# Issuing the last batch's output rows inside the branch's other arm

## The chip, the cores and the metric

The kernel runs on one core of a Trainium2 chip. The metric is the time of one execution on the device, in microseconds, as the median of several runs. A core has five engines with an instruction queue each: PE (matmul), DVE (vector), ACT (scalar), POOL (GpSimd) and SP, which here only issues transfers. The engines wait for each other through semaphores, counters that an instruction or a transfer raises when it is done.

## What is computed

Attention in which a query sees only the keys of its own cluster, followed by an MLP mixer over tokens and channels, all in float32; 4 batches, 8 heads, 768 tokens, 64 values for a head, 16 clusters, 256 hidden values over tokens, 1536 over channels:

```python
q_assign = np.argmax(np.einsum('bhsd,hcd->bhsc', q_n, c_n), axis=-1)
k_assign = np.argmax(np.einsum('bhsd,hcd->bhsc', k_n, c_n), axis=-1)
mask = q_assign[:, :, :, None] == k_assign[:, :, None, :]
scores = np.where(mask, scale * np.matmul(q, k.transpose(0, 1, 3, 2)), -1000000000.0)
...
x = attn_out.transpose(0, 2, 1, 3).reshape(B, S, H * D)
h = np.maximum(x.transpose(0, 2, 1) @ w_tok1, 0.0) @ w_tok2
u = x + h.transpose(0, 2, 1)
return u + np.maximum(u @ w_ch1, 0.0) @ w_ch2
```

## The kernel before

The kernel has a fast path and a general one. The fast path takes shortcuts that hold only for inputs like those given (each query and key with one clear nearest cluster, sums of exponentials within bounds); it checks this while it runs. `fits` and `fits_count` leave three counts in a small tile, `fits_load` (L1000) loads them into registers of every engine, and their sum is `both`. When the fast path's program has ended, each engine compares `both` with 3 * 128 at L1382. If it is smaller, the engine falls through into the code of `general()`, which computes the whole output again in a plain way: some thousands of instructions, 383 of them on SP. Otherwise it jumps over them into the other arm. In the kernel before that arm is empty in the source. The framework still puts instructions there: each engine waits until its own counters have the value of the fast path's end and raises them to the value that the general path would have left, so that what follows can wait for the same numbers. For SP these are eight waits, one for each of the eight counters of its transfers. Then all engines come to the program's end (shown under L1407), where SP waits for all transfers and all engines, and the engines exchange two rounds of semaphores.

The fast path works through the attention for pairs of heads, then through the token part of the mixer for pairs of batches, then through the channel part for one batch after the other, in the order 0, 2, 3, 1. The channel part of a batch has three parts; each has a product up (`ch1_pair`, L799, L812) and a product back down (`ch2_chunks`, L952), both in Winograd's form with seven products of blocks. `by_turns` goes through the products of a part in an order written out by hand: a product on PE into a PSUM bank, then an add on DVE (L565) of that bank onto the batch's tile `xs[b]`. That tile holds 128 partitions with six rows (`j` of 0 to 5) of 512 values each, so that one row is 256 KB over all partitions. The output goes out by rows: `out_row(j)` at L962 issues one transfer from SP.

For the first three batches the six rows are issued together after the third part. For the last batch, which is batch 1, `by_turns` calls `done` after each add; where the product was `c12` or `c21`, the add was the last one to that row, and `done` issues the row. The order of the products at the end is c12 0, c12 1, c11 2, c12 2, c22 0, c22 1, c21 0, c22 2, c21 1, c21 2, so the rows are done as 0 to 5 and the sixth with the last add of the program. SP, whose queue runs in order, thus has at the end: the loads of the counts, six issues that each wait for an add, the comparison and the branch.

The registers are loaded for the last part only, ahead of its `ch2_chunks`; on SP that is right after the third batch's rows.

The tile of the last batch lies in the pool `xpool`. It is opened on the stack `fast`, which is closed ahead of the branch so that the general path can use the space.

Of the kernel before, what the change touches and what calls it, by code (L numbers as in the profile page):

```python
# [19 lines left out]
P = 128  # L20
NJ = S // P
DM = H * D
# [5 lines left out]
HJ = NJ // 2  # L28
# [22 lines left out]
def kernel(  # L51
# [29 lines left out]
    nc = tc.nc  # L81
# [5 lines left out]
    def pool(name, bufs, stack=None, **kw):  # L87
        return (stack or fast).enter_context(
            tc.tile_pool(name=name, bufs=bufs, reuse_waits="tile", **kw)
        )  # L90
# [2 lines left out]
    ps_sc_stack = fast.enter_context(ExitStack())  # L93
    ps_sc = pool("ps_sc", 3, ps_sc_stack, space=PSUM)

    xpool = pool("xpool", 1)
    wc1pool = pool("wc1pool", 1)
    tokens = fast.enter_context(ExitStack())
    x1pool = pool("x1pool", 1, tokens)
# [34 lines left out]
    xs = [(x1pool if b == 1 else xpool).tile([P, NJ, DM], F32, name=f"x{b}") for b in range(B)]  # L134
# [386 lines left out]
    def ptile(tag, n):  # L521

        if tag == "Y":
            return ps_av.tile([P, n], F32, tag="av", name="pY")
        return pools["ps_m"].tile([P, n], F32, tag=tag, name="p" + tag)
# [38 lines left out]
    def add(dst, a, b):  # L564
        nc.vector.tensor_tensor(out=dst, in0=a, in1=b, op=ALU.add)  # L565
# [171 lines left out]
    def between(n=1):  # L737
        if late:
            late.pop(0)()
        for _ in range(min(n, len(others))):  # L740
            others.pop(0)()

    def by_turns(n, product, of, done=None, last=False, after=()):


        if last:
            order = "p1 0 p1 1 p1 2 p5 0 p5 1 p5 2 c11 0 c11 1 u2 0 u2 1 u2 2 c12 0 c12 1 c11 2 c12 2 "
            order += "c22 0 c22 1 c21 0 c22 2 c21 1 c21 2"
        else:
            order = "p1 0 p1 1 p1 2 p5 0 p5 1 p5 2 c11 0 c11 1 u2 0 u2 1 u2 2 c12 0 c12 1 "  # L750
            order += "c22 0 c22 1 c22 2 c12 2 c11 2 c21 0 c21 1 c21 2"
        order = order.split()
        banks, after = {}, dict(after)
        for m in range(len(order) // 2):
            name, i = order[2 * m], int(order[2 * m + 1])
            tag, a, r, to = SEVEN[name]
            if name in FIRST:
                banks[tag, i] = ptile(tag, n)
            product(banks[tag, i], a, r, i, name in FIRST)
            x = of(to, i)  # L760
            add(x, banks[tag, i], x)
            if done:
                done(name, i)
            if m in after:
                after[m]()
            between()

    def tok2_chunks(b, after=()):

        A, R = pools["AT"], pools["RT"]  # L770

        def product(psum, a, r, i, start):
            nc.tensor.matmul(  # L773
                psum, lhsT=A[a][:, i], rhs=R[r], start=start, stop=True,
                skip_group_check=not start,
            )

        def of(to, i):
            return xs[b + int(to[2]) - 1][:, HJ * (int(to[1]) - 1) + i]

        by_turns(DM, product, of, after=after)

    def ch1_pair(part, sets, beside):
# [147 lines left out]
        else:  # L931
            sum_1()

            def late_(i):
                product(X[i], "A22", "T4", i, False)
                nc.scalar.activation(out=a12[:, i], in_=X[i], func=ACT.Relu)
                if i == 0:
                    sub(h2["S2"], h2["S1"], a11)
                else:
                    sum_3()  # L940
                    sum_4()

            late_(0)
            late.append(lambda: late_(1))

    def ch2_chunks(b, part, last, after=()):

        h2, Bw = pools["h2"], pools["B"]

        def product(psum, a, w, i, start):  # L950
            for k in range(2):
                nc.tensor.matmul(  # L952
                    psum, lhsT=h2[a][:, k, i * P : (i + 1) * P], rhs=Bw[w][:, part + 3 * k],
                    start=start and k == 0, stop=k == 1, skip_group_check=not start,
                )

        def of(to, i):
            r, c = int(to[1]) - 1, int(to[2]) - 1
            return xs[b][:, HJ * r + i, 256 * c : 256 * c + 256]

        def out_row(j):
            nc.sync.dma_start(out[b].rearrange("(p j) m -> p j m", p=P)[:, j], xs[b][:, j])  # L962

        def done(name, i):
            if name in ("c12", "c21"):
                out_row(i + HJ * (name == "c21"))

        by_turns(DM // 2, product, of, done if last else None, last, after)
        if part == 2 and not last:
            for j in range(NJ):  # L970
                out_row(j)

    good = const.tile([P, 3], F32, name="good")
    count = const.tile([1, 3], I32, name="count")
# [22 lines left out]
    def fits_load():  # L997

        loaded = [
            nc.values_load(count[0:1, i : i + 1], min_val=0, max_val=P) for i in range(3)  # L1000
        ]
        return loaded[0] + loaded[1] + loaded[2]
# [155 lines left out]
    batches = (0, 2, 3, 1)  # L1158
    for n, b in enumerate(batches):
        turning = []  # L1160
        for part in range(3):
            first, last = n == 0 and part == 0, n == B - 1 and part == 2
# [15 lines left out]
            if last:  # L1178
                both = fits_load()
            after = {}  # L1180
            if part == 2 and not last:
                after[3] = lambda: take(turning, len(turning))
                after[15] = lambda: next(usums)
                usums = u_sums()
            ch2_chunks(b, part, last, after)
            between(len(others))
            if n == 0 and part < 2:
# [191 lines left out]
        gctx.close()  # L1379

    fast.close()
    with tc.If(both < 3 * P):  # L1382
        general()
# [1 line left out]
_INS = ['q', 'k', 'v', 'centroids', 'moe_w_tok1', 'moe_w_tok2', 'moe_w_ch1', 'moe_w_ch2']  # L1385
_OUTS = [((B, S, DM), 'float32')]
# [25 lines left out]
```

## Time and profile before

| what | value |
|---|---|
| median of 4 runs | 829.24 us (828.43 to 829.69) |
| device time of the profiled execution | 829.55 us |
| its span, from the first to the last instruction | 827.7 us |
| mean granted TensorE clock | 0.999 |
| output transfers from L962 | 24 of 256 KB each, median 2.5 us to landing |
| last six issues on SP, start of the first and the last | 813.94, 821.71 us |
| issue time of these six: shortest, median, longest | 332, 333, 1010 ns |
| their landing times: shortest, median, longest | 2.0, 2.0, 3.0 us |

The profiled execution is one run; its device time holds the span and 1.85 us around it. In lines of the profile a small q behind an engine's name (SPq, DVEq) means its sequencer: register, branch, semaphore and transfer-issuing instructions, which don't count as busy time. A group "x8: 17/17/17, 825.8 to 826.3" has eight instructions, shortest, median and longest duration in ns, and the starts of the first and the last in us from the span's start. "DMA to landing" is the time from the start of a transfer's issue to the last increment of its counter. A line of waits reads: who waited, for whom, us in total, times, longest.

### The profile page before, as it was taken

Reading aid. Unit: us, or ns where it says so; the run is one execution under the profiler, and the core shown is the slowest. Engines: PE = TensorE matmul, PEld = TensorE weight load, DVE = VectorE, ACT = ScalarE, POOL = GpSimd, SP = SyncE. Lnnn points to the kernel's source line nnn. Section 1 sums busy time; section 2 is a strip of 40 time slices with the busy share of each in tenths; the row PEclk is TensorE's granted clock in tenths of the full one; section 3 lists DMA queues with packets and bytes.
Section 4 is the critical chain, followed back from the end, with each engine's and each line's share of the span. In section 5 each row is a group of like instructions: output and inputs, shape, how many; then the busy total and the mean of one; then the engine's idle time right before and its main releaser. Section 6 shows DMA issues by size and latency. Waiting matters only on the chain.

```text
span 827.7 us, 11453 instructions
## 1 busy us (share of the span) xinstructions
PE 818.3 (99%) x4282; PEld 526.4 (64%) x4282; DVE 605.2 (73%) x1124; ACT 381.4 (46%) x562; POOL 30.7 (4%) x28
## 2 busy tenths in 40 slices
PE   8999999999999999999999999999999999999996
PEld 4444444444444444444688787878878788787875
DVE  6879898989898968859777687654677456674654
ACT  5588777787878775136202253121541214512020
POOL 1001010111101000000000000000000000000000
PEclk9999999999999999999999999999999999999999
DMA  9797665767676434143000114000130001400002
GB/s 154 140 164 143 128 141 121 157 141 155 139 155 142 84 96 121 51 156 48 0 1 1 29 34 168 1 0 15 35 105 1 1 1 31 122 1 0 1 2 80
DMA packets 184256, 63.39 MB, mean 77 GB/s; under 512 B 172800, under 2 KB 176896, under 8 KB 183936
## 3 DMA queue, kind: packets, MB, share of 16 engines
q1 hardware_dynamic: 182592, 62.18, 34.7%
q8 instruction: 35, 0.57, 0.3%
q10 hardware_dynamic: 1600, 0.39, 0.2%
q14 instruction: 29, 0.24, 0.1%
HBM read 36.21 MB, written 7.86 MB: 53 GB/s over the span
## 4 chain that ended last, share of the span: by engine, by line
PE 95%; DVE 4%; ACT 0%; issue 0%; ACTq 0%; DVEq 0%
PE sc L413 19%; PE av L455 15%; PE pX L952 14%; PE pX L799 11%; PE pZ L952 7%; PE ph L534 5%; PE pY L812 4%; PE pY L952 4%; PE pZ L799 3%; PE pZ L812 3%; PE pX L773 2%; PE pX L812 2%; PE small L491 2%; PE pZ L773 1%; PE small L304 1%; DVE hA L565 1%
## 5 line engine op out<-in xcount | busy, mean ns | idle before, releaser
L437 ACT ACTIVATE ex<-sc 128x768 f32<-128x768 f32 x192 | 151.0, 812 | 27.2 <-PE sc L413 15.5
L413 PE MATMUL sc<-qkT 64*128 64x384 f32 x768 | 155.3, 483 | 0.0
L445 DVE TENSOR_TENSOR sum<-sum,ex 128x768 f32<-128x768 f32 x128 | 127.8, 998 | 27.5 <-ACT ex L437 15.4
L455 PE MATMUL av<-ex,va 128*64 128x384 f32 x768 | 127.4, 488 | 0.0
L565 DVE TENSOR_TENSOR x<-pX,x 128x256 f32<-128x256 f32 (+1 forms) x168 | 76.0, 459 | 40.9 <-PE pX L952 40.4
L455 PEld LDWEIGHTS av<-ex,va 128*64 128x64 f32 x768 | 53.7, 137 | 71.7 <-issue 67.2
L413 PEld LDWEIGHTS sc<-qkT 64*128 64x128 f32 x768 | 67.8, 187 | 38.3 <-issue 38.0
L839 ACT COPY hA<-pX 128x384 f32<-128x384 f32 x24 | 11.5, 479 | 146.0 <-PE pX L799 146.0
L565 DVE TENSOR_TENSOR hA<-pY,hA 128x192 f32<-128x192 f32 (+1 forms) x90 | 36.7, 408 | 50.0 <-PE pY L812 36.0
L821 ACT ACTIVATE hA<-hA 128x768 f32<-128x768 f32 x35 | 29.5, 843 | 87.1 <-DVE hA L565 87.1
L799 PE MATMUL pX<-uT,wc 128*128 128x384 f32 x192 | 67.9, 487 | 0.0
L413 PE MATMUL sc<-ohT 64*128 64x384 bf16 x384 | 62.4, 323 | 0.0
L799 PEld LDWEIGHTS pX<-uT,wc 128*128 128x128 f32 x192 | 35.8, 190 | 17.5 <-issue 0.4
L462 ACT COPY avrows<-av 128x768 uint16<-128x768 uint16 x32 | 25.6, 799 | 44.0 <-PE av L455 44.0
L565 DVE TENSOR_TENSOR x<-pZ,x 128x256 f32<-128x256 f32 (+1 forms) x84 | 36.4, 455 | 11.9 <-PE pZ L952 11.9
L534 PE MATMUL ph<-x,wt 128*128 128x512 f32 x96 | 41.6, 593 | 0.0
L413 PEld LDWEIGHTS <-ohT 64*128 64x128 bf16 x384 | 18.7, 94 | 33.8 <-issue 9.6
L952 PE MATMUL pX<-wc,hA 128*128 128x256 f32 x144 | 36.9, 380 | 0.4 <-ACT hA L897 0.4
L708 ACT COPY uT<-ucols 128x768 uint16<-128x768 uint16 x32 | 33.2, 1050 | 4.5 <-DMA ucols<-urows 4.5
L952 PE MATMUL pY<-wc,hA 128*128 128x256 f32 x144 | 35.1, 379 | 0.0
L952 PE MATMUL pZ<-wc,hS 128*128 128x256 f32 x144 | 35.0, 379 | 0.0
L799 PE MATMUL pX<-uTs,w1s 128*128 128x384 f32 x96 | 34.9, 486 | 0.0
(178 smaller groups left out, 1266.2 us busy)
## 6 DMA issues: line engine op xcount, KB each, us to landing
raw<-in_moe_w_ch_dram SPq DMA_DIRECT2D x24, 512.0 KB, 4.4
va<-in_v_dram SPq DMA_DIRECT2D x16, 384.0 KB, 3.5
out_dram<-x SPq DMA_DIRECT2D x24, 256.0 KB, 2.5
qk<-in_k_dram SPq DMA_DIRECT2D x60, 96.0 KB, 3.9
qk<-in_q_dram SPq DMA_DIRECT2D x60, 96.0 KB, 3.5
raw<-in_moe_w_tok_dram SPq DMA_DIRECT2D x3, 512.0 KB, 4.3
raw<-in_moe_w_tok_dram SPq DMA_DIRECT2D x4, 384.0 KB, 4.1
spill<-x SPq DMA_DIRECT2D x1, 1536.0 KB, 5.1
```

The costliest lines, as they stand in the source:

```text
L413: nc.tensor.matmul(sc[:, h, 0:HS], lhsT=src[rows, 1, j], rhs=src[rows, 0, HJ * qh : HJ * qh + HJ], start=start, stop=not start,)
L437: nc.scalar.activation(out=ex, in_=sc[:, :, 0:HS], func=ACT.Exp, scale=SM_SCALE)
L445: nc.vector.tensor_tensor(out=acc, in0=acc if j > 1 else st["ex", qh, 0], in1=st["ex", qh, j], op=ALU.add)
L455: nc.tensor.matmul(av[h * D : (h + 1) * D], lhsT=st["va"][:, h, j], rhs=ex[:, h], start=(j == 0), stop=(j == NJ - 1),)
L462: nc.scalar.copy(out=st["rows"][:, qh], in_=av.bitcast(U16).rearrange("p (t w) -> p w t", w=2))
L534: nc.tensor.matmul(pf, lhsT=W["tok1"][:, j, t * P : (t + 1) * P], rhs=xs[b][:, j], start=(j == 0), stop=(j == NJ - 1),)
L565: nc.vector.tensor_tensor(out=dst, in0=a, in1=b, op=ALU.add)
L708: nc.scalar.copy(out=out, in_=pools.pop(("ucols", i)).rearrange("p w j t -> p w (j t)"))
L799: nc.tensor.matmul(psum, lhsT=A[a][:, k, c], rhs=R[r][:, k], start=start and k == 0, stop=k == 1, skip_group_check=not start,)
L812: nc.tensor.matmul(psum, lhsT=left[which][a][:, part * P : part * P + P], rhs=right[which][r], start=start, stop=True, skip_group_check=no ...
L821: nc.scalar.activation(out=x, in_=x, func=ACT.Relu)
L952: nc.tensor.matmul(psum, lhsT=h2[a][:, k, i * P : (i + 1) * P], rhs=Bw[w][:, part + 3 * k], start=start and k == 0, stop=k == 1, skip_grou ...
```

## The change

The six row transfers of the last batch no longer stand in the fast path's program between the adds. They stand in the arm of the branch that is taken when the fast path's checks held. `done` and the test of the product's name go away, `out_row` becomes a function of batch and row, and the pool of the last tile is kept open until the end of the kernel, so that the tile may still be read in the arm. The general path, when it runs, writes all four batches itself, as before.

In the built program, SP's part before the branch is shorter by twelve instructions (six transfers, six waits), and its arm grows from 9 instructions to 21. For each row the arm has a wait that raises the row's counter to the other arm's value, less what the row itself will add, then the wait on the same counter, then the transfer, which waits for the same count of DVE's adds as before. Two waits for the two counters that no row uses follow. At the program's end SP's first of eight waits is for the counter of the sixth row and, as before, its sixth asks for DVE's counter too, which DVE raises in its own arm.

```diff
-    xpool = pool("xpool", 1)
+    xpool = pool("xpool", 1, ctx)
...
-    def by_turns(n, product, of, done=None, last=False, after=()):
+    def by_turns(n, product, of, last=False, after=()):
...
-            if done:
-                done(name, i)
...
+    def out_row(b, j):
+        nc.sync.dma_start(out[b].rearrange("(p j) m -> p j m", p=P)[:, j], xs[b][:, j])
+
...
-        def out_row(j):
-            nc.sync.dma_start(out[b].rearrange("(p j) m -> p j m", p=P)[:, j], xs[b][:, j])
-
-        def done(name, i):
-            if name in ("c12", "c21"):
-                out_row(i + HJ * (name == "c21"))
-
-        by_turns(DM // 2, product, of, done if last else None, last, after)
+        by_turns(DM // 2, product, of, last, after)
         if part == 2 and not last:
             for j in range(NJ):
-                out_row(j)
+                out_row(b, j)
...
-    with tc.If(both < 3 * P):
+    with tc.If(both < 3 * P) as fit:
         general()
+    with fit.Else():
+
+        for j in range(NJ):
+            out_row(batches[-1], j)
```

## The prediction

> **What bounds the kernel now.** I read the page's first two parts, to see which engine fills the span and at which clock.
>
> ```profile
> span 827.7 us, 11453 instructions
> PE 818.3 (99%) x4282; PEld 526.4 (64%) x4282; DVE 605.2 (73%) x1124; ACT 381.4 (46%) x562; POOL 30.7 (4%) x28
> PEclk9999999999999999999999999999999999999999
> ```
>
> TensorE is busy for 99% of the span, at a granted clock that stays in the top tenth in every slice. The change touches no matmul and no vector instruction; in the built changed program the four compute engines have, ahead of the branch, the same instructions in the same order with the same waits and the same addresses. So nothing before the last stage can move. What can move is the end: TensorE is done near 821.2, the span ends at 827.7, and the 6.5 us between them belong to something else. So next I read the chain of waits of the last stretch and its timeline.
>
> ```profile
> 816.04 5.20 PE pX L952 x24
> 821.23 0.02 issue
> 821.26 0.42 DVE x L565
> ...
> 813.94 8.78 SPq L962 DMA_DIRECT2D out_dram<-x  x6
> ...
> 821.71 1.01 SPq L962 DMA_DIRECT2D out_dram<-x  x1
> ```
>
> The chain ends with the last add on DVE (821.26 to 821.68). Its row, the sixth, is issued by SP at 821.71. That issue holds SP for 1.01 us; the page's view of this line gives 332 to 333 ns as minimum and median of the six. Then the line of the branch itself, and what SP waited for.
>
> ```profile
> L1382 SPq EVENT_SEMAPHORE  x8: 17/17/17, 825.8 to 826.3; - x8
> L1382 PEldq COMPARE_BRANCH  x1: 3779/3779/3779, 820.1 to 820.1; - x1
> L1382 DVEq COMPARE_BRANCH  x1: 72/72/72, 821.4 to 821.4; - x1
> L1382 SPq COMPARE_BRANCH  x1: 58/58/58, 822.9 to 822.9; - x1
> L1382 PEldq EVENT_SEMAPHORE  x1: 51/51/51, 823.9 to 823.9; - x1
> L1382 DVEq EVENT_SEMAPHORE  x1: 21/21/21, 824.3 to 824.3; - x1
> ...
> SPq L1382 <- SPq L1382: 2.9, 1, 2.9
> ...
> L1407 SPq EVENT_SEMAPHORE  x8: 27/28/28, 826.4 to 826.8; - x8
> ...
> DMA to landing us min/median/max: 2.8/2.8/2.8
> ```
>
> This is the bound of the tail. SP compares and jumps at 822.9, and its first instruction in the arm that is taken comes at 825.8: for 2.9 us it waits for nothing but itself. The same gap stands behind the branches of DVE (821.4 to 824.3, 2.9), PE (820.1 to 823.9, 3.8, booked as the branch's own time) and ACT (806.4 to 808.8, 2.4); on POOL, with the shortest program, it is 0.5 (467.7 to 468.2). I read it as the time to load the code of a far target. Meanwhile the sixth row, issued at 821.71 and landing 2.8 us later (last line), has been in memory since 824.5. SP then does eight waits in the arm (825.8 to 826.3), eight at the program's end (826.4 to 826.8) and the closing exchange between the engines, which ends at 827.7. So SP, not the row, sets the end: the jump starts only when the last row has been issued.
>
> **The change, part by part.**
>
> *The six issues move behind SP's branch.* They are the same six transfers of 256 KB in the same order, each waiting for the same count of DVE's adds. What they are moved past is SP's two branch instructions; no other queue is passed, and behind SP's last load of the counts (716.7, all done by about 717.2 on SP) nothing else stands on SP in this program. So SP can jump at about 717.3. The first row is wanted at 813.94. A code load of 2.9 us, or PE's 3.8, would be over by 721.1, which leaves 92 us of cover. That cover is the work of the last batch on PE; without it the first row would be late by the 2.9 us.
>
> *What the arm adds.* Ahead of each row stand a wait that also raises the row's transfer counter to what the other arm would have left, and the wait that was there before. A wait with such a raise takes about 0.07 us from start to start in the trace (eight in 825.8 to 826.3). The fifth issue ends at 821.2 (820.84 and 0.33), the sixth starts at 821.7: two waits, 0.15 us, fit into that half microsecond while DVE does the last add. So they cost nothing; with no gap they would cost 0.15.
>
> *What is taken off the path.* After the sixth issue (end 822.7) SP has two more catch-up waits (0.15) and reaches the program's end at about 822.9. There the first of the eight waits is the one on the sixth row's counter. SP stands there until that row has landed, and the rest of the tail follows as now: from the first of these waits to the end of the span it took 827.7 - 826.4 = 1.3 us. The landing thus takes the place of the code load as what SP waits for last.
>
> *The price of the landing.* It is in the trace: 821.71 + 2.8 = 824.5. From below: the shortest of the last six took 2.0, which would be 823.7. From above: the longest, the fifth row, took 3.0, which would be 824.7. The fast ones had issues of 0.33 us and no other load around; the fifth and the sixth lie inside PE's and DVE's code loads, which stay where they are. So I take the 2.8 of the very same transfer and keep both ends.
>
> *The next engine in line.* Of the eight last waits, the sixth also asks for DVE's mark, and DVE makes it in its own arm at 824.3, after its own jump. That jump cannot go earlier, since it stands behind the last add. In the present run SP's sixth wait is at about 826.7 (826.4 and five steps of 0.06). So even a row that lands at once cannot bring more than 826.7 - 824.35, about 2.35 us. PE's mark, at 823.9, is behind that.
>
> *The pool in another stack.* `xpool` now lives until the kernel's end, so the six rows may still be read in the arm. In the built program the addresses of the main part are unchanged; the general path reuses less memory, and that path doesn't run. Cost nothing.
>
> **The sum**, on the profiled execution: first end wait from 826.4 to 824.5, that is 1.9 us; 0.1 off for the step from the counter's last increment to the wait and for rounding, so 1.8. Span 827.7 to 825.9; device time 829.55 to 827.75. That execution lies 0.31 above the median of the runs (829.24), so the median goes to 827.4, 0.22% less.
>
> The row says that a jump costs 2.9 us on SP, 58 ns for the instruction and the rest for what follows. [...]
>
> [...]
>
> **Rivals.**
>
> *DVE becomes the last one.* The sixth issue took 1.01 us instead of 0.33. If that came from SP's own state before the jump, the row lands by 823.7 to 824.0, and DVE's mark at 824.3 decides. For it: five of six issues took 0.33. Against it: the issue falls into PE's code load (820.1 to 823.9), as does the fifth row with its 3.0 us. Gain 2.35: 826.9.
>
> *A second code load at the end.* If the code behind the arm isn't there yet, SP pays the load again after the sixth issue: 822.7 + 0.15 + 2.9 = 825.8 instead of 826.4, a gain of 0.6, time 828.6. Against it: in this trace SP goes from its arm (last wait 826.3) to the end (826.4) without a gap, and it has 92 us to load ahead. That the change doesn't do what it says (SP not jumping early) would leave 829.2; the order of the built program speaks against it, so I put it in with this case.
>
> *The slower side.* The arm's code is loaded in pieces, a piece ends just before the sixth row, and the next is fetched only when SP gets there. Then the issue starts at 821.2 + 2.9 = 824.1 and the row lands 2.0 to 3.0 later, at 826.1 to 827.1, against the present first end wait at 826.4: with 2.8, 826.9, which is 0.5 slower, 829.7; with PE's load of 3.8 another 0.9, 830.6. The point from which it decides: an issue later than 826.4 - 2.8 = 823.6. For it: the arm is now 21 instructions of SP instead of 9. Against it: no gap of this kind stands in SP's straight code before the branch; the five first rows were issued 0.03 us after their adds.
>
> **How the numbers follow.** The landing decides: 0.60, time 827.4, own range 827.0 to 827.8. DVE decides: 0.22, 826.9. A second load or no early jump: 0.13, 828.6 to 829.2. Slower: 0.05, 829.7 to 830.6. The bounds of the landing give 826.9 to 827.6, the scatter of the runs before (828.43 to 829.69) some 0.4 on either side, and the upper end is drawn up to the second load: 826.5 to 828.6. A measurement of this kernel tells about 0.2%, 1.66 us, from no change. DVE's case is over it whole; of the landing's some two thirds: 0.22 + 0.42, about 0.65 faster. Slower by more than that needs both high ends of the last case and is kept at 0.04; the rest, 0.31, is within.
>
> **What would show it.** SP's branch at about 717 and its arm's first wait some 3 us later; six issues at the same times as now (813.9 to 821.7); no gap of 2.9 us on SP after 821; the first end wait passing within 0.1 us of the sixth row's landing, near 824.5; a span of 825.4 to 826.1. The prediction is wrong if an issue starts more than 0.1 us after its add, if SP shows a gap between the sixth issue and the end that isn't the landing, or if PE's or DVE's jump takes longer than 3.8 and 2.9 us.

## The result and the profile after

The changed kernel takes 827.74 us (median of 31 runs, 826.87 to 828.21), the kernel before 829.05 (51 runs, 828.36 to 829.69). The ratio is 0.9984, with a 95% interval of 0.9979 to 0.9989: 1.3 us faster, 0.16%, with an interval of about 0.9 to 1.7 us. Against 827.4 as predicted the sign is right and the gain is smaller than the 1.8 us of the sum.

The page of the changed kernel, first its span and its busy times, is nearly the same for the engines and 2.5 us shorter as a span:

```profile
span 825.2 us, 11453 instructions
PE 817.8 (99%) x4282; PEld 526.0 (64%) x4282; DVE 605.2 (73%) x1124; ACT 381.5 (46%) x562; POOL 30.7 (4%) x28
```

The end of its timeline:

```profile
813.57 8.46 SPq L945 DMA_DIRECT2D out_dram<-x  x6
...
820.89 0.42 DVE L565 TENSOR_TENSOR x<-pX,x 128x256 f32<-128x256 f32 x1 [0.44 <-PE pX L953]
```

The view of the branch's line, now L1376:

```profile
L1376 SPq EVENT_SEMAPHORE  x2: 17/17/17, 822.1 to 822.1; - x2
...
L1376 SPq COMPARE_BRANCH  x1: 58/58/58, 717.2 to 717.2; - x1
...
L1376 PEldq COMPARE_BRANCH  x1: 3461/3461/3461, 819.8 to 819.8; - x1
...
L1376 DVEq COMPARE_BRANCH  x1: 72/72/72, 821.0 to 821.0; - x1
L1376 PEldq EVENT_SEMAPHORE  x1: 51/51/51, 823.3 to 823.3; - x1
L1376 DVEq EVENT_SEMAPHORE  x1: 21/21/21, 824.0 to 824.0; - x1
```

The view of the end's line, now L1405, which in this kernel also names the arm's first waits, in a window from 719 us:

```profile
L1405 SPq EVENT_SEMAPHORE  x1: 17/17/17, 719.9 to 719.9; - x1
```

And what SP's queue waited for in the last 6 us:

```profile
SPq L945 <- DVE x L565: 3.7, 3, 2.1
SPq L1405 <- DMA out_dram<-x: 1.7, 1, 1.7
SPq L1405 <- PEq L1405: 0.6, 2, 0.5
```

SP jumps at 717.2 and its arm begins at 719.9: the gap costs 2.7 us there, 94 us ahead of the first row. The prediction read such a gap as the load of the target's code, and the traces bear it out. From 717.2 to 719.9 the DMA queues of the changed kernel move a single packet, of 8 KB, on an instruction queue (queue, packets, MB, share of the time):

```profile
q14 instruction: 1, 0.01, 1.3%
```

It runs from 718.2 to 718.7. In the kernel before, where SP jumps later, nothing moves from 717.0 to 719.9. In all fourteen traces an instruction packet starts 0.9 to 1.5 us behind each jump of SP, ACT, DVE and PE; POOL, which jumps over 69 instructions, has none in its gap and goes on after 0.5 us.

At the end the wait of SP for itself is gone from the list; in its place SP waits 1.7 us for a transfer, from 822.2 to 823.9. That is the sixth row, issued at 821.3 and landed 2.5 us later, as the view of its line shows; SP's end waits (second fence, the end's line again) begin right behind that:

```profile
L945 SPq DMA_DIRECT2D out_dram<-x x1: 689/689/689, 821.3 to 821.3; - x1
...
DMA to landing us min/median/max: 2.5/2.5/2.5
```

```profile
L1405 SPq EVENT_SEMAPHORE  x9: 17/28/28, 823.9 to 824.6; - x9
```

The last add ends at 821.31 and the span 3.86 us later; in the kernel before it was 6.05 us. So the two profiled executions differ by 2.2 us in this tail alone, and yet the median time falls by 1.3. Where the rest went was the question for the runs. The work ahead of the tail shows no shift: the last add ends between 820.9 and 822.1 in the six traces of the kernel before and its variants, and between 821.3 and 821.8 in the four traces in which no row of the last batch stands ahead of the branch.

### The profile page after: what moved, and what is told of

Same layout as the page of the kernel before. It is cut to its first block, busy times and chain, and to the rows that moved or that the text cites. A ratio compares the mean times of both kernels' runs of the same rounds, so it can differ in the third digit from the quotient of the medians.

```text
span 825.2 us, 11453 instructions
## 1 busy us (share of the span) xinstructions
PE 817.8 (99%) x4282; PEld 526.0 (64%) x4282; DVE 605.2 (73%) x1124; ACT 381.5 (46%) x562; POOL 30.7 (4%) x28
## 4 chain that ended last, share of the span: by engine, by line
PE 95%; DVE 4%; ACT 0%; issue 0%; ACTq 0%; DVEq 0%
PE sc L413 19%; PE av L455 15%; PE pX L953 15%; PE pX L797 11%; PE pZ L953 7%; PE ph L534 5%; PE pY L810 4%; PE pY L953 4%; PE pZ L797 3%; PE pZ L810 3%; PE pX L771 2%; PE pX L810 2%; PE small L491 2%; PE pZ L771 1%; PE small L304 1%; DVE hA L565 1%
```

## The experiments

All but three runs were timed in five rounds beside the kernel before. Each run has a time and a span; "outside" is the median of time less span. The ratio is to the kernel before in the same rounds, where its median was 829.12, 829.09 or 828.98; it is not the quotient of the two medians.

| run | time | span | outside | ratio to the kernel before |
|---|---|---|---|---|
| before (33 runs) | 829.12 | 827.3 | 1.78 | |
| changed (31 timed runs) | 827.74 | 825.7 | 2.02 | 0.9984 [0.9979, 0.9989] |
| before, again | 829.46 | 827.7 | 1.75 | 1.0001 [0.9992, 1.0010] |
| changed, again | 827.49 | 825.6 | 2.00 | 0.9979 [0.9970, 0.9988] |
| sixth row alone in the arm | 830.44 | 828.5 | 2.01 | 1.0017 [1.0008, 1.0026] |
| fifth and sixth in the arm | 830.70 | 828.7 | 1.95 | 1.0011 [1.0002, 1.0020] |
| changed, no sixth row | 827.43 | 825.2 | 2.28 | 0.9980 [0.9971, 0.9989] |
| before, no sixth row | 828.12 | 826.7 | 1.47 | 0.9987 [0.9978, 0.9996] |
| before, pool kept open | 829.39 | 827.4 | 2.04 | 1.0002 [0.9993, 1.0011] |
| changed, last half row alone | 827.62 | 825.6 | 2.06 | 0.9983 [0.9974, 0.9992] |
| before, no fifth row | 828.42 | 826.7 | 1.72 | 0.9994 [0.9985, 1.0003] |

### Both kernels once more

The kernel before, unchanged:

> The kernel before, once more, for a second look at its tail and for spans beside its times. Theory A (SP's jump at the end pays a code load that nothing hides; the sixth row lands under it): again a gap of 2.9 us on SP between its branch and its arm, the sixth row landed at least 1 us before SP's arm begins; device time 829.05 within 0.3. Rival B (the gap is a chance of one execution, and the landing is usually the last): a gap under 2 us, with the arm's first wait released by the row. On the small size of the gain (1.3 us measured, 2.5 between the two profiled spans): if time less span is again near 1.85 us against 2.0 in the changed kernel's runs, 0.15 us of it lies outside the spans; if it is 2.0 here too, all of it lies in the spans.

In the second trace of the kernel before SP's arm begins at 826.0, 2.7 us after its branch, and the sixth row has landed at 825.0. The median, 829.46, is 0.1 over the expected 829.05 ± 0.3. Time less span is 1.75 and 1.78. Theory A holds in its main point: a load that nothing hides, and the row under it. Beside the changed kernel's 2.0 the time less span also shows that 0.25 us of what the spans gain is missing in the times.

The changed kernel, unchanged:

> The changed kernel once more, beside the others on one chip. Theory A: span 825.7 within 0.2, time outside it 2.0; the first of SP's end waits is released by the sixth row's landing, with no gap of another kind on SP after 821; tail from the end of the last add to the end of the span between 3.8 and 4.4 us, against 6.0 in the kernel before.

The span's median is 825.6, the time outside 2.00, and SP's wait at the end is again for the transfer (1.6 us). The tail is 825.8 less the end of the last add at 821.83, 3.9 us.

### A late jump: one or two rows in the arm

```diff
...
+        def done(name, i):
+            j = i + HJ * (name == "c21")
+            if name in ("c12", "c21") and j < 5:
+                out_row(b, j)
+
-        by_turns(DM // 2, product, of, last, after)
+        by_turns(DM // 2, product, of, done if last else None, last, after)
...
-        for j in range(NJ):
+        for j in range(5, NJ):
             out_row(batches[-1], j)
```

> Five rows are issued before the branch, the sixth alone in the arm. Theory A: SP can jump only after the fifth issue (ends 0.5 us before the last add is done), so the load of 2.9 us delays the sixth issue by some 2.4 us, and its landing of 2.0 to 2.8 us follows in full: first end wait between 0.3 before and 0.5 us after that of the kernel before, time 828.8 to 829.6, that is 1.1 to 1.9 us over the changed kernel. Rival B (an early jump isn't what counts, only that the arm's eight waits come in another place): 827.7, as the changed kernel.

It is 830.44, slower than the kernel before, and 0.8 us over the upper end of what was expected. The trace shows what theory A says. First the timeline, then what SP waited for, then the sixth issue and its landing:

```profile
820.71 3.93 SPq L947 DMA_DIRECT2D out_dram<-x  x2
821.12 0.42 DVE L565 TENSOR_TENSOR x<-pX,x 128x256 f32<-128x256 f32 x1 [0.44 <-PE pX L955]
```

```profile
SPq L1412 <- SPq L1412: 2.9, 1, 2.9
SPq L1412 <- DMA out_dram<-x: 1.7, 1, 1.7
```

```profile
L947 SPq DMA_DIRECT2D out_dram<-x x1: 340/340/340, 824.3 to 824.3; - x1
...
DMA to landing us min/median/max: 2.5/2.5/2.5
```

The two waits that the other kernels have one of stand here one behind the other: 2.9 us for the code, 1.7 for the row. The sixth issue comes 2.8 us after its add, which ended at 821.5. In this trace the first end wait comes 5.3 us after the last add (826.8 less 821.5), against 4.7 in the first trace of the kernel before. Of the 0.8 us over the expectation, 0.23 lies outside the span (2.01 against 1.78). The rest is probably that the expectation was made, as the prediction had been, from the tail of one execution of the kernel before, which was a long one, as the traces below show. Rival B falls: the last row in the same kind of arm, but with a jump at 821.2 instead of 717.2, makes the kernel 2.7 us slower than the changed one.

The same with `j < 4` and `range(4, NJ)`:

> Four rows before the branch, the fifth and the sixth in the arm. Theory A: SP jumps after the fourth issue, 2.2 us before the last add is done, and the load ends some 0.7 us after it; fifth and sixth are issued one behind the other, the sixth about 1.1 us late: first end wait 0.8 to 1.3 us later than in the changed kernel, time 828.4 to 828.9. Rival B: 827.7.

The median is 830.70, over the expected 828.4 to 828.9, but the spans of the 11 runs fall into two groups: four between 826.2 and 827.2, seven between 827.9 and 829.2. The first trace belongs to the lower group, with a jump 2.1 us before the last add's end, a load of 2.7 us and a sixth issue 1.3 us late, which is what theory A asks. Two more traces of it, to meet the other group:

> The kernel with the fifth and sixth row in the arm, again: its spans fall into two groups, 826.2 to 827.2 and 827.9 to 829.2, and the first trace is of the lower one (first end wait 3.97 us after the last add). If this one is of the upper group, theory A says that one of its two loads or the landing is longer: the arm's first instruction more than 2.8 us after SP's jump, or the sixth row's landing more than 2.7 us after its issue, by 1 to 2 us in all. Rival E (SP waits at the end for the code of the next block, which isn't there yet): a gap of 1 to 2 us on SP between two instructions that wait for nothing, behind the sixth issue.

> The same kernel once more, for a trace of the other group. Theory A: a longer load behind SP's jump or a longer landing of the sixth row, 1 to 2 us. Rival E: a gap of 1 to 2 us on SP behind the sixth issue in which it waits for nothing.

Spans of 826.7 and 827.1: both of the lower group, with loads of 2.9 and 2.7 us and landings of 2.6. So the upper group was never traced, and neither the longer load nor rival E is tested. What makes this kernel some 2 us slower in most of its executions is open.

### What comes next on the path

The changed kernel with the loop in the arm cut to `range(NJ - 1)`, so that the sixth row isn't written:

> The changed kernel without the transfer of the last batch's sixth row, which is left out of the output. Theory A with DVE as the next in line: DVE's mark (824.0 in the changed kernel's trace) is wanted by SP's sixth end wait, which stood at 824.2 there, so no more than 0.2 us can be won: 827.5 to 827.7, and SP's sixth end wait is released by DVE. Rival C (the landing alone sets the end, DVE has room): the fifth row lands 0.6 us ahead of the sixth, so 827.1.

The time is 827.43, the span 825.2, 0.5 under the changed kernel. SP's longest wait is now one for DVE's mark, as its queue's waits and the end's line show (this run's L1376 and L1405 are the branch and the end):

```profile
SPq L1405 <- DVEq L1376: 2.6, 1, 2.6
```

```profile
L1405 SPq EVENT_SEMAPHORE  x9: 17/28/2620, 821.2 to 824.5; - x9
```

DVE is next, and behind the sixth row by little: 0.3 us of time, 0.5 of span. Rival C falls.

The kernel before with the test in `done` narrowed so that the sixth row isn't written:

> The kernel before without the transfer of the last batch's sixth row, which is left out of the output. Theory A (in the kernel before SP's own order, last issue, jump, code load, arm, sets the end, and the landing lies under it): SP jumps after the fifth issue, some 1.5 us earlier, and every step up to the end moves with it until DVE's mark decides: span 1.4 to 1.6 us shorter, the gap on SP behind its branch again 2.9 us. Rival C (the last landing sets the end of the kernel before): the fifth row lands 0.7 us ahead of the sixth, so the span is 0.7 us shorter.

SP's branch is at 821.5, before the end of the last add at 821.9, and its first end wait at 825.1, 3.2 us after that add instead of 4.7. This is the 1.5 us of theory A. The span is only 0.6 shorter, though, and the view of the end's line shows why:

```profile
L1407 SPq EVENT_SEMAPHORE  x10: 17/28/28, 825.1 to 826.3; - x10
...
L1407 PEldq EVENT_SEMAPHORE  x2: 51/51/51, 825.8 to 826.3; - x2
L1407 DVEq EVENT_SEMAPHORE  x2: 21/21/21, 825.8 to 827.0; - x2
```

All engines do the last step of the closing exchange at 826.3, only DVE at 827.0, without a wait that the profile names. In return 0.3 us less lies outside. The time falls by 1.0. That DVE waits there for code is a guess. What speaks for it: an instruction packet ends at 825.7, 1.3 us ahead of DVE's late step, and behind SP's jump in the changed kernel the first instruction came 1.2 us after the end of its packet. Whose packet it is isn't shown. Rival C's 0.7 in the span is near the 0.6 seen, but for a reason that is not its own.

### The other half of the change alone

```diff
-    xpool = pool("xpool", 1)
+    xpool = pool("xpool", 1, ctx)
```

in the kernel before, and nothing else:

> The kernel before with the pool of the last tile kept open, the other part of the change alone. If the time outside the span (1.78 us before, 2.02 in the changed kernel) grows because the built general path is a few instructions shorter and everything behind it has moved in each engine's code, it is near 2.0 here too, and the time 0.2 us over the kernel before. If it grows because SP jumps early, it stays at 1.78 and the time is that of the kernel before, 829.1 within 0.3. In both cases the span is 827.3 within 0.3.

The span stays (827.4), and the time outside it goes from 1.76, in the runs of the kernel before beside it, to 2.04. So the 0.25 us outside the span come with the pool, not with the early jump. The sixth row moves this time too, in opposite directions: without it, it is 2.28 in the changed kernel and 1.47 in the kernel before. The built general path, which doesn't run, is four DVE instructions and three PE instructions shorter, and all code behind it stands that much earlier. The trace's list of packets goes on past the span's end: an instruction packet starts 0.65 us behind it in the five traces with the pool closed (the kernel before three times, and without the fifth or the sixth row) and 1.8 to 2.1 us behind it in the nine with the pool open. So code is still loaded there, and at another moment. That the time ends later because of this load isn't shown. As a ratio of times (1.0002) this is within noise; only time less span resolves it.

### What made the kernel before's tail long or short

A third trace of the kernel before:

> The kernel before, a third trace of its tail. The first two have 6.05 and 5.86 us from the end of the last add to the end of the span, with a gap of 2.9 and 2.8 us on SP behind its branch. If the span's median fell by only 1.6 us (827.3 to 825.7) because this tail is often shorter, it is near 5.5 us here; if the tail is steady and the time up to the last add varies, it is 5.8 to 6.2 us, with the last add ending between 820.5 and 822.2.

Here the tail is 5.3 us (826.7 less 821.4), and SP's issue of the sixth row differs (first fence). In the run with the pool kept open, whose rows stand before the branch as well, it is long again, with a tail of 6.1 us (second fence):

```profile
L963 SPq DMA_DIRECT2D out_dram<-x x1: 332/332/332, 821.5 to 821.5; - x1
...
DMA to landing us min/median/max: 2.9/2.9/2.9
```

```profile
L962 SPq DMA_DIRECT2D out_dram<-x x1: 1110/1110/1110, 821.5 to 821.5; - x1
...
DMA to landing us min/median/max: 3.0/3.0/3.0
```

The row lands equally late in both, but SP is free 0.8 us earlier in the first, and jumps that much earlier. In the four traces with six rows before the branch, issues of 1.01, 0.95, 1.11 and 0.33 us stand beside tails of 6.0, 5.9, 6.1 and 5.3. To see what holds the issue, the kernel before with the fifth row left out of the output:

```diff
-            if name in ("c12", "c21"):
+            if name in ("c12", "c21") and i + HJ * (name == "c21") != 4:
```

> The kernel before without the transfer of the last batch's fifth row, which is left out of the output. In four traces of the kernel before's last rows the sixth issue held SP for 1010, 947, 1110 and 332 ns, and the span's end followed it (6.05, 5.86, 6.14 and 5.30 us after the last add). Theory F (the issue is held up by the fifth row's transfer, which is still on its way beside PE's code load): with that transfer gone the issue takes 0.33 us in every run, and the spans draw together near 826.7, 0.6 under the kernel before's median of 327.3 + 500, that is 827.3. Rival G (PE's code load alone holds it up): issue near 1.0 us again in most runs, span 827.3 within 0.3.

The span's median is 826.7, against 827.2 for the kernel before in the same rounds, and the trace has the short issue:

```profile
L962 SPq DMA_DIRECT2D out_dram<-x x1: 332/332/332, 821.0 to 821.0; - x1
```

and SP's wait behind its branch as in the others:

```profile
SPq L1382 <- SPq L1382: 2.7, 1, 2.7
```

PE's code load is still there (its branch takes 3.8 us from 819.4). That fits theory F: the fifth row's transfer, under way beside PE's load, is what holds SP. By itself it rests on one trace and on the spans, which didn't draw together (826.0 to 827.0, beside 826.6 to 827.7); by times alone the run is the same as the kernel before (0.9994, interval up to 1.0003).

The packets in the kept traces say more. In each of the five traces with a long sixth issue (the three above, and the changed kernel's two with 0.69 and 0.81 us) a packet of 16 KB on the other instruction queue, about 1 us behind PE's branch, starts 0.2 to 0.3 us after the start of the fifth issue, while SP is still in it; and the sixth issue ends 0.4 us after that packet has ended. In the kernel before's third trace the packet starts 0.8 us after the start of the fifth issue, and the sixth takes 0.33 us. So it isn't enough that row and load are both under way; in these traces the hold goes with a load that starts right behind the row.

### A version that might be faster

```diff
...
-        for j in range(NJ):
-            out_row(batches[-1], j)
+        out_row(batches[-1], slice(0, HJ))
+        out_row(batches[-1], 3)
+        out_row(batches[-1], 5, slice(DM // 2, DM))
+        out_row(batches[-1], 4)
+        out_row(batches[-1], 5, slice(0, DM // 2))
```

> The changed kernel with the rows 0 to 2 as one transfer and the sixth row in two halves, of which the right one is issued an add earlier; the last transfer is 128 KB, and its counter is the last of SP's eight end waits. Theory A with DVE next in line: the seven other waits are done while the last half is on its way, the landing is about 0.3 us earlier, and the end is set by DVE's mark in the sixth wait; span 0.2 to 0.5 us under the changed kernel's 825.7, time 827.2 to 827.6. Rival D (descriptors of half the size land no earlier, and the order of the waits doesn't matter): 827.7.

It takes 827.62, against 827.49 for the changed kernel in the same rounds; the spans are equal at 825.6. The trace has SP waiting for DVE:

```profile
SPq L1410 <- DVEq L1378: 1.8, 1, 1.8
```

so the row is off the path, and the tail is 3.7 us instead of 3.9. That is too little to be seen in the times. No version was found that beats the changed kernel.

## Why the prediction was right, and where it was short

*The bound.* SP's jump behind the last issue, with a code load of 2.9 us over the landing of the row: shown by the late-jump run, in which the load moved in front of the sixth issue and the kernel became slower than before, and by the kernel before without a sixth row, in which SP came to its end waits 1.5 us earlier. The branch instruction itself took 58 ns on SP, and the gap behind it was 2.5 to 2.9 us in every traced run.

*The early jump.* SP jumps at 717.2 as worked out (717.3), and its load of 2.7 us is under the last batch. The arm's extra waits cost nothing: the sixth issue starts 0.03 us after its add. The profiled span, 825.2, lies 0.2 under the 825.4 to 826.1 that was to show the theory; the median, 825.7, lies within.

*The landing as the next bound.* It is: SP's first end wait passes at 823.9, when the row has landed. Its price was put at 2.8 us; 2.5 and 2.6 were measured, which is 0.2 to 0.3 in the change's favour. Between 2.0 and 3.3 us were measured for the last six rows in the traces of both kernels.

*DVE next.* Its mark follows 0.1 us behind the landing in the changed kernel's trace, and decides as soon as the row is taken away or made smaller. The 0.22 given to it as a separate case was too fine a distinction: the two cases lie within 0.5 us of span.

*The second code load and the slower side.* Neither came; no gap of SP stands behind 821 other than the landing. The late-jump run shows that the price of the slower side was real: an issue 2.8 us after its add loses to the kernel before.

*The sum was too large, by two of its terms.* The step that failed is the one that made the sum "on the profiled execution" and carried it over to the median. First, that execution had the sixth issue at 1.01 us, and in the kernel before SP's issue time lies straight on the path to the jump. The prediction saw the 1.01 beside 0.33 and weighed it for the landing alone. In the third trace of the kernel before the issue took 0.33 and the tail 5.3 us; against the changed kernel's 3.9 that is a gain of 1.4, and not the 2.2 of the profiled pair. The median of the spans falls by 1.6, between the two. How many executions are of which kind isn't shown; three of the four traced ones, the run with the pool kept open among them, had the long issue. Second, the device time was taken to fall by as much as the span. It falls by 0.25 less, and the pool's line alone brings that. The term "cost nothing" for the pool is therefore wrong by 0.25 us. Together 1.6 - 0.25 gives the 1.3 that was measured. So the gain stays under the 0.2% that the chances drew as a line, and the 0.65 for "faster by more than that" was too much. That 827.4 comes as near to 827.74 as it does is in part luck: on the profiled pair the tail gained 0.4 us more than the sum's 1.8, and that made up for some of what the two terms took away.

Open: why the kernel with two rows in the arm has a second, slower group of spans, what DVE waited for at the end of the kernel before without a sixth row, and what lies in the 0.25 us outside the span.

## What to carry to other kernels

In these traces SP, which jumps over the 383 instructions of its general path, went on only 2.5 to 2.9 us after its jump, with an instruction packet under way in the gap; if an engine with such a gap is idle before its last task, let it jump first and do the task behind the branch, where the gap is covered (here by 94 us). Do it with all of the task: a part left before the branch ties the jump to that part, and the gap then lies in front of what is left (830.44 us with one row left for the arm, 830.70 with two, against 827.74 with all six). And before a term of a microsecond is taken from one execution, look in the same trace at whether instructions of its kind vary by as much, and where such a variation lies on the path.

## What was not expected of the hardware

The time that SP needs to issue the same 256 KB transfer wasn't fixed. Rows issued 0.86 us or more apart mostly took 0.33 us; the first batch's six in the kernel before, issued one right behind the other, took 0.42 to 0.63 us each. The last batch's sixth row, one add behind the fifth, held SP for 0.7 to 1.1 us in five of six traces, and then its issue ended 0.4 us after a 16 KB instruction packet that had started during the fifth issue. And a change in code that never runs changed the time: with four DVE and three PE instructions less in it, time less span rose from 1.76 to 2.04 us.
